# Rational layer's last units: f32 output product and another order of the element-wise steps

## The chip, the cores and the metric

One core of one Trainium2 chip runs the whole program as a single launch. The metric is the time on the device in microseconds (us). The engines are TensorE (PE, with its weight loads PEld), VectorE (DVE), ScalarE (ACT), GpSimd (POOL) and SyncE (SP).

## The reference, cut to what matters

```python
X = np.fft.fft(np.fft.fft(x, axis=1), axis=2).real      # x: 8 x 3072 x 256
x = X.reshape(24576, 256)
# mixture of 8 experts, one expert for each row, F = 1024
out[mask] = gate_w[mask, None] * (np.maximum(xe @ w1[e], 0.0) @ w2[e])
# rational layer
h = x @ w_in                                            # 256 -> 2048
P = a[0] + a[1] * h + a[2] * h2 + a[3] * h3
Q = 1.0 + np.abs(b[0]) * np.abs(h) + np.abs(b[1]) * h2
return (P / (Q + 1e-06)) @ w_out                        # 2048 -> 256
```

## The kernel before

After the transform and the sorting of rows by expert come two layers that run interleaved. The expert layer works in 103 blocks of 256 rows, each block in four "pieces" (two for the first product, two for the second). The rational layer works in 96 blocks of 256 rows, each in four "units" of 512 hidden columns, counted here by their place in the list `units`, 0 to 384; the last one is cut into two halves, 383 and 384. One round of the main loop issues one unit and one piece. The pieces end before unit 376, the value of `free`, so that units 376 to 384 have the engines to themselves: this is the stretch that the change touches, with 376 itself only at its border.

A unit i has these steps. `m2a(i)`: PE forms the hidden tile h (24 matmuls of 256 columns, f16 in high and low parts) in PSUM; ACT reads h three times, for a scaled absolute value (Abs), a square (Square) and a linear function (Identity); POOL adds the first two to q; DVE makes the numerator with two operations on the linear factor u and h (L1314, L1315). `m2b(i)`: ACT takes the logarithm of q (Ln) and its reciprocal (Exp, L1324), which it writes over h in PSUM; DVE finishes with three operations (L1325 to L1327). `m2g(i)`: ACT rounds the result to f16 (`ghi`), POOL makes the rest (`glo`). `m2c(i)`, three rounds later: PE multiplies both by the f16 parts of the output weights (24 matmuls of 256 columns) into the accumulator `po`; after a block's last unit `po` goes to `o` and by an indirect DMA to the output.

What sets the order is the text: the schedule is written by hand, each engine takes its instructions in that order, and waits are put in from what is read and written. h lives in one of three PSUM places: two turns of the tag `h2`, which units 376, 377, 378, 380, 381, 383 and 384 use, and one of the tag `h1` (units 379 and 382). So the matmuls of 378 reuse the place of 376, two units earlier, and those of 380 and later units the place of three units earlier. The u tiles by number: u__47327 is unit 376, u__47395 is 377, u__47478 is 378, u__47554 is 379, u__47627 to u__47765 are 380 to 382, u__47829 and u__47890 the halves 383 and 384.

Of the kernel before, what the change touches and what calls it, by code (L numbers as in the profile page):

```python
# [10 lines left out]
F32 = mybir.dt.float32  # L11
# [3 lines left out]
AF = mybir.ActivationFunctionType  # L15
ALU = mybir.AluOpType
# [4 lines left out]
P = 128  # L21
S = 3072
D = 256
# [108 lines left out]
def fourier_moe_rational_kernel(ctx, tc, xl, wg, w1, w2, w_in, w_out, av, bv, cst, out):  # L132
    nc = tc.nc
    V = nc.vector
# [23 lines left out]
    wslot = [keep.tile([P, wrow], F16, name=f"wslot{i}") for i in range(2)]  # L158
# [82 lines left out]
    with ExitStack() as c1:  # L241
# [53 lines left out]
        fs = spare[0][0:B, 1792:2816].rearrange("p (t c) -> p t c", t=4)  # L295
# [470 lines left out]
        for s in range(NS):  # L766
            p = s - 1
# [22 lines left out]
            else:  # L790
                parts = stage1_odd(b, eo, 3)
# [54 lines left out]
            parts = None  # L846
            if s and jh == 0:
                parts = stage1_odd(b, eo, 2)
# [29 lines left out]
        p = NS - 1  # L878
# [30 lines left out]
        for e in range(E):  # L909
            q = (nc.sync, nc.scalar)[e % 2]  # L910
            v = q.value_load(runi[0:1, e:e + 1], min_val=e * R, max_val=e * R + NT)
            ins_z.append(q.dma_start(out=xs[ds(v, TB), :], in_=cst["c_z"]))
        for i in ins_z:
# [25 lines left out]
                        op=ALU.is_ge)  # L939
# [7 lines left out]
                               op0=ALU.mult, op1=ALU.add)  # L947
# [10 lines left out]
        def places(k, end):  # L958
# [32 lines left out]
                        in1=sm[:, 8:16].unsqueeze(1).to_broadcast(bl), op=ALU.is_equal)  # L991
# [25 lines left out]
    wout = kp.tile([P, 2, 16, D], F16, name="wout")  # L1017
# [125 lines left out]
    st = {}  # L1143
# [40 lines left out]
    def three(ps, wa, wb, xa, xb):  # L1184

        n = len(wa)
        for i in range(n):
            nc.tensor.matmul(ps, lhsT=wa[i], rhs=xa[i], start=i == 0, stop=False)  # L1188
            nc.tensor.matmul(ps, lhsT=wb[i], rhs=xa[i], start=False, stop=False)  # L1189
        for i in range(n):  # L1190
            nc.tensor.matmul(ps, lhsT=wa[i], rhs=xb[i], start=False, stop=i == n - 1)  # L1191
# [95 lines left out]
        V.reciprocal(out=ir, in_=r)  # L1287
        nc.gpsimd.tensor_scalar(out=oj_, in0=ir, scalar1=ir, scalar2=og, op0=ALU.mult, op1=ALU.mult)

    def m2a(j, u, fs=range(4)):  # L1290
        yt = st["y", j][0]

        i = 4 * j + u + np_ - 4 * NSB + (fs[0] > 0)
        own = i < 1 or i % 3
        n = len(fs)
        ps = (psH if own else psM).tile([P, 4, TB], F32, tag="h2" if own else "h1", name="h2")[:, 0:n]
        for f in fs:
            fo = (4 * u + f) * P
            three(ps[:, f - fs[0]], [win[:, 0, kc, fo:fo + P] for kc in range(2)],
                  [win[:, 1, kc, fo:fo + P] for kc in range(2)],  # L1300
                  [yt[:, kc] for kc in range(2)], [yt[:, 2 + kc] for kc in range(2)])
        ab_ = tp.tile([P, 4, TB], F32, tag="ab", name="ab_")[:, 0:n]
        sq_ = tp.tile([P, 4, TB], F32, tag="sq", name="sq_")[:, 0:n]
        if i < 0:
            u_ = tp.tile([P, 4, TB], F32, tag="u", name="u_")
        else:

            u_ = bp.tile([P, 8, TB], F16, tag=("hhi", "hlo")[i % 2], name="u_")
            u_ = u_.rearrange("p f t -> p (f t)").bitcast(F32).rearrange("p (f t) -> p f t", t=TB)[:, 0:n]
        nc.scalar.activation(out=ab_, in_=ps, func=AF.Abs, scale=kb0)  # L1310
        nc.scalar.activation(out=sq_, in_=ps, func=AF.Square, scale=kb1)
        nc.scalar.activation(out=u_, in_=ps, func=AF.Identity, scale=ka3, bias=ka2)
        (V if fs[0] else nc.gpsimd).tensor_tensor(out=sq_, in0=sq_, in1=ab_, op=ALU.add)
        V.tensor_tensor(out=u_, in0=u_, in1=ps, op=ALU.mult)  # L1314
        V.scalar_tensor_tensor(out=u_, in0=u_, scalar=ka1, in1=ps, op0=ALU.add, op1=ALU.mult)  # L1315
        st["r", j, u, fs] = (ps, sq_, u_)

    def m2b(j, u, fs=range(4)):
        ps, q_, w_ = st["r", j, u, fs]
        n = len(fs)  # L1320
        L = tp.tile([P, 4, TB], F32, tag="L", name="L")[:, 0:n]
        nc.scalar.activation(out=L, in_=q_, func=AF.Ln, bias=c1b)

        nc.scalar.activation(out=ps, in_=L, func=AF.Exp, scale=-1.0, bias=st["bnd", j][3])  # L1324
        V.scalar_tensor_tensor(out=w_, in0=w_, scalar=a0, in1=ps, op0=ALU.add, op1=ALU.mult)  # L1325
        V.scalar_tensor_tensor(out=ps, in0=q_, scalar=C1, in1=ps, op0=ALU.add, op1=ALU.mult)  # L1326
        V.scalar_tensor_tensor(out=w_, in0=ps, scalar=st["bnd", j][5], in1=w_, op0=ALU.subtract, op1=ALU.mult,  # L1327
                               reverse0=True)

    def m2g(j, u, fs=range(4)):  # L1330
        ps, q_, w_ = st.pop(("r", j, u, fs))
        n = len(fs)
        ghi = tp.tile([P, 4, TB], F16, tag="ghi", name="ghi", bufs=3)[:, 0:n]
        glo = tp.tile([P, 4, TB], BF16, tag="glo", name="glo", bufs=3)[:, 0:n]
        nc.scalar.activation(out=ghi, in_=w_, func=AF.Copy)  # L1335
        (V if fs[0] else nc.gpsimd).tensor_tensor(out=glo, in0=w_, in1=ghi, op=ALU.subtract)  # L1336
        st["g", j, u, fs] = (ghi, glo)

    def m2c(j, u, fs=range(4)):
        ghi, glo = st.pop(("g", j, u, fs))  # L1340
        if u == 0:
            st["po", j] = psM.tile([P, 2, D], F32, tag="po", name="po")
        ps = st["po", j]
        for g, parts in ((ghi, (0, 1)), (glo, (0,))):
            for f in fs:
                for q in range(2):
                    for h in parts:
                        nc.tensor.matmul(ps[:, q], lhsT=g[:, f - fs[0], q * P:(q + 1) * P], rhs=wout[:, h, 4 * u + f],  # L1348
                                         start=g is ghi and u == 0 and f == 0 and q == 0 and h == 0,
                                         stop=g is glo and u == 3 and f == 3, skip_group_check=True)  # L1350
        if u == 3 and fs[-1] == 3:
            o = bp.tile([P, 2, D], F32, tag="o", name="o")
            oj_ = st.pop(("bnd", j))[7]
            t = st.pop(("y", j))[1]
            if j < NB - 1:
                nc.scalar.activation(out=o, in_=ps, func=AF.Copy, scale=oj_)
            else:
                V.tensor_scalar(out=o[:, 0], in0=ps[:, 0], scalar1=oj_, scalar2=None, op0=ALU.mult)
                nc.scalar.activation(out=o[:, 1], in_=ps[:, 1], func=AF.Copy, scale=oj_)
            for q in range(2):  # L1360
                ins = nc.gpsimd.indirect_dma_start(  # L1361
                    out=out, out_offset=bass.IndirectOffsetOnAxis(ap=t[:, q:q + 1], axis=0),
                    in_=o[:, q], in_offset=None, bounds_check=NT - 1, oob_is_err=False).ins
                tc.declare_no_dep(ins, group="out", reason="every token has a row of its own")
                tc.add_to_no_dep_group("out", ins)

    def piece(i, first=False):

        j, s_ = divmod(i, 4)
        if j >= NSB:  # L1370
            return
        if s_ == 0:
            pairs(j + 1, 1)
        if s_ < 2:
            m1a(j, s_, first)
        else:
            m1b(j, s_ - 2, first)
        if s_ == 3:
            pairs(j + 2, 0)
        if s_ == 3 and j + 2 < NSB:  # L1380
            gather(j + 2)
        if s_ == 1 and j + 1 < NSB:
            transp(j + 1)
        if s_ == 1 and j + 3 < NSB:
            load(j + 3)
# [34 lines left out]
    units = [(j, u) for j in range(NB) for u in range(4)]  # L1420
    last = units.pop()
    units += [(*last, range(2)), (*last, range(2, 4))]
    free = 4 * NSB - np_
    CL = 3
    for i in range(len(units) + CL + 1):

        lag = 1 + (i > free)
        if i == len(units):
            m2g(*units[i - lag])
        if 1 <= i <= len(units):  # L1430
            m2b(*units[i - 1])
        if i == len(units) - 1:
            m2g(*units[i - lag])
        if i < len(units):
            j, u = units[i][:2]
            if i == 0:
                piece(np_)
            m2a(*units[i])
            if i < len(units) - 1:
                if i:  # L1440
                    piece(i + np_)
                if u == 1 and j + 1 < NB:
                    bound_sum(j + 1)
                if u == 3 and j + 1 < NB:
                    bound_scale(j + 1)
                if u == 1 and j + 1 < NB:
                    load_y(j + 1)
        if i not in (free + 1, len(units) - 1, len(units)) and lag <= i < len(units) + lag:
            m2g(*units[i - lag])
        if i < len(units) - 1:  # L1450
            if u == 1 and j + 1 < NB:
                bound(j + 1)
            if u == 3 and j + 2 < NB:
                bound_rows(j + 2)
            if u == 1 and j:
                bound_out(j)
        if CL <= i < len(units) + CL:
            m2c(*units[i - CL])
# [35 lines left out]
```

## Time and profile before

| what | value |
|---|---|
| median of 3 runs | 3513.91 us (3513.57 to 3516.85) |
| profiled execution: time, span | 3516.32 us, 3514.6 us |
| busy over the span: PE, DVE, ACT, POOL | 96%, 87%, 89%, 80% |
| mean granted TensorE clock | 0.984 of full speed |

The span runs from the first to the last instruction of the profiled execution; the time holds in addition what lies around it. Busy shares are averages over the whole span, and say nothing of the last units by themselves.

### The profile page before, as it was taken

The page shows a single profiled execution, that of the slowest core. Times are in us where ns is not written, and L with a number is a line of the kernel's source. Part 1 is how long each engine was busy: PE and PEld are TensorE (multiplying, and loading weights), DVE is VectorE, ACT ScalarE, POOL GpSimd, SP SyncE. Part 2 cuts the span into 40 slices and gives each one's busy share as a digit, 9 for nine tenths or more (in the row PEclk, how much of TensorE's full clock was granted, in tenths as well). Part 3 has the DMA queues.
Part 4 walks back from the last instruction along what each step waited for, and adds up shares of the span by engine and source line. Part 5 has one row for each costly group of instructions (what it writes and reads, how often), then busy time and mean ns, then how long its engine had stood idle before and what let it go on. Part 6 is the DMA issues. An engine that isn't in the chain of part 4 may idle for free.

```text
span 3514.6 us, 75025 instructions
## 1 busy us (share of the span) xinstructions
PE 3391.1 (96%) x29902; PEld 2968.8 (84%) x29902; DVE 3044.7 (87%) x3214; ACT 3123.4 (89%) x3904; POOL 2824.1 (80%) x2552
## 2 busy tenths in 40 slices
PE   7984989999999999999999999999999999999997
PEld 5663778888888888888888888888888888888885
DVE  9986668888988889888988889888898888888897
ACT  4774479999999999999999999999999999999997
POOL 2887668888888888888888888888888888888876
PEclk9996999999999999999999999999999999999999
DMA  8987423111321123111221123111311123212110
GB/s 298 305 274 261 105 43 93 38 43 45 67 70 40 43 43 94 39 45 43 67 69 40 42 45 93 44 40 43 91 46 40 44 43 91 46 40 43 44 31 19
DMA packets 344639, 268.32 MB, mean 76 GB/s; under 512 B 182470, under 2 KB 319686, under 8 KB 337232
## 3 DMA queue, kind: packets, MB, share of 16 engines
q1 hardware_dynamic: 311136, 182.50, 21.7%
q0 software_dynamic: 33024, 79.96, 6.6%
q8 instruction: 234, 3.83, 0.6%
q14 instruction: 117, 0.96, 0.2%
q10 hardware_dynamic: 128, 1.06, 0.1%
HBM read 327.00 MB, written 96.92 MB: 121 GB/s over the span
## 4 chain that ended last, share of the span: by engine, by line
PE 88%; DVE 4%; ACT 2%; issue 2%; DMA 2%; POOL 1%; POOLq 0%; SPq 0%; ACTq 0%; DVEq 0%
PE po L1348 28%; PE h L1189 14%; PE h L1188 14%; PE h L1191 14%; PE py L1191 5%; PE py L1188 5%; PE py L1189 5%; POOL xs L612 1%; DMA xs<-y,sli 1%; PE ps L507 1%; PE pq L531 1%; PE ps L480 1%; PE pq L532 1%; DVE h L1326 0%; ACT h L1324 0%
## 5 line engine op out<-in xcount | busy, mean ns | idle before, releaser
L1188 PE MATMUL h<-yr,win 128*128 128x256 f16 x3072 | 755.7, 273 | 8.9 <-DVE u__5102 L1327 5.6
L1189 PE MATMUL h<-yr,win 128*128 128x256 f16 x3072 | 755.7, 273 | 0.0
L1348 PE MATMUL po<-wout,ghi 128*128 128x256 f16 x6144 | 735.1, 273 | 11.2 <-ACT ghi L1335 7.6
L1348 PEld LDWEIGHTS <-ghi 128*128 128x128 f16 x6144 | 593.6, 98 | 81.7 <-ACT ghi L1335 12.0
L1191 PE MATMUL h<-yr,win 128*128 128x256 f16 x3072 | 587.5, 273 | 0.0
L1324 ACT ACTIVATE h<-L,bnd 128x1024 f32<-128x1024 f32 x385 | 429.6, 1116 | 20.9 <-DVE u__47829 L1315 1.5
L1188 PE MATMUL h<-xt,wslot 128*128 128x256 f16 x1648 | 406.3, 274 | 2.5 <-DVE hlo L1214 1.7
L1189 PE MATMUL h<-xt,wslot 128*128 128x256 f16 x1648 | 406.3, 274 | 0.0
L1348 PE MATMUL po<-wout,glo 128*128 128x256 f16 x3072 | 399.3, 273 | 1.8 <-POOL glo L1336 1.8
L1188 PE MATMUL py<-hhi,wslot 128*128 128x256 f16 x1648 | 373.4, 274 | 3.5 <-ACT hhi L1208 3.5
L1189 PE MATMUL py<-hhi,wslot 128*128 128x256 f16 x1648 | 373.3, 274 | 0.0
L1189 PEld LDWEIGHTS <-wslot 128*128 128x128 f16 x3296 | 323.5, 98 | 45.1 <-issue 6.9
L1188 PEld LDWEIGHTS <-wslot 128*128 128x128 f16 x3296 | 323.3, 98 | 39.1 <-issue 0.4
L1191 PEld LDWEIGHTS <-wslot 128*128 128x128 f16 x3296 | 323.1, 98 | 38.5 <-issue 0.3
L1188 PEld LDWEIGHTS <-win 128*128 128x128 f16 x3072 | 300.7, 98 | 45.5 <-DVE u__5102 L1327 5.7
L1348 PEld LDWEIGHTS <-glo 128*128 128x128 bf16 x3072 | 300.4, 98 | 38.4 <-POOL glo L1336 3.2
L1189 PEld LDWEIGHTS <-win 128*128 128x128 f16 x3072 | 301.0, 98 | 35.2
L1191 PEld LDWEIGHTS <-win 128*128 128x128 f16 x3072 | 300.8, 98 | 35.2
L612 POOL DMA_INDIRECT xs<-y,sli x192 | 225.5, 1175 | 117.1 <-ACT L L535 58.5
L1191 PE MATMUL h<-xt,wslot 128*128 128x256 f16 x1648 | 315.8, 273 | 0.0
L1214 DVE SCALAR_TENSOR_TENSOR hlo<-h,hhi 128x1024 f16<-128x1024 f32 x197 | 240.0, 1218 | 29.1 <-ACT hhi L1208 24.1
L1361 POOL DMA_INDIRECT out_dram<-o,id x192 | 199.3, 1038 | 53.7 <-issue 47.3
(4924 smaller groups left out, 9119.7 us busy)
## 6 DMA issues: line engine op xcount, KB each, us to landing
xr<-xs SPq DMA_DIRECT2D x103, 258.0 KB, 2.9
ys<-yw SPq DMA_DIRECT2D x103, 256.0 KB, 5.5
yr<-ys SPq DMA_DIRECT2D x96, 256.0 KB, 3.8
xh<-x_l SPq DMA_DIRECT2D x14, 1536.0 KB, 9.2
wf<-in_moe_w_dram SPq DMA_DIRECT2D x16, 1024.0 KB, 6.6
ws<-wh SPq DMA_DIRECT2D x16, 1024.0 KB, 12.1
xh<-in_moe_w_in_dram SPq DMA_DIRECT2D x4, 1024.0 KB, 5.9
wslot<-ws SPq DMA_DIRECT2D x4, 1024.0 KB
```

What stands on the lines that cost most here:

```text
L480: nc.tensor.matmul(ps[0:m, 0:n], lhsT=eo[i][:, jh, c], rhs=mat[:, c, 0:n], start=c == 0, stop=c == 2)
L507: nc.tensor.matmul(ps[q][0:m, 0:NH], lhsT=eo[i][:, c], rhs=mat[:, c], start=c == 3 * q, stop=c == 3 * q + 2)
L531: nc.tensor.matmul(pq[:, k, 0:NC], lhsT=u[2 * par][:, js], rhs=rc, start=True, stop=False)
L532: nc.tensor.matmul(pq[:, k, 0:NC], lhsT=u[2 * par + 1][:, js], rhs=rs, start=False, stop=True)
L612: ins = nc.gpsimd.indirect_dma_start(out=xs, out_offset=bass.IndirectOffsetOnAxis(ap=sli[:, t0 + t:t0 + t + 1], axis=0), in_=y[:, t], in_o ...
L1188: nc.tensor.matmul(ps, lhsT=wa[i], rhs=xa[i], start=i == 0, stop=False)
L1189: nc.tensor.matmul(ps, lhsT=wb[i], rhs=xa[i], start=False, stop=False)
L1191: nc.tensor.matmul(ps, lhsT=wa[i], rhs=xb[i], start=False, stop=i == n - 1)
L1214: V.scalar_tensor_tensor(out=hlo[:, sl], in0=ps, scalar=0.0, in1=hhi[:, sl], op0=ALU.max, op1=ALU.subtract)
L1324: nc.scalar.activation(out=ps, in_=L, func=AF.Exp, scale=-1.0, bias=st["bnd", j][3])
L1348: nc.tensor.matmul(ps[:, q], lhsT=g[:, f - fs[0], q * P:(q + 1) * P], rhs=wout[:, h, 4 * u + f], start=g is ghi and u == 0 and f == 0 and ...
L1361: ins = nc.gpsimd.indirect_dma_start(out=out, out_offset=bass.IndirectOffsetOnAxis(ap=t[:, q:q + 1], axis=0), in_=o[:, q], in_offset=None, ...
```

## The change

For the units after 376 three things differ. The result of a unit is no longer split: the f32 tile u goes into the output product as it is, against f32 weights `w32`, which POOL adds up from the two f16 parts in four operations (`widen`) in rounds 376 to 379, into the weight slot that the last odd expert block has left. ACT forms the linear factor first, DVE makes the numerator from it at once, and only then comes Abs. Between Abs and Square of unit i stands the whole of `m2b(i - 1)`, which before stood ahead of `m2a(i)`.

```diff
@@ m2a @@
+        st["r", j, u, fs] = (ps, sq_, u_)
+
+        def numerator():
+            V.tensor_tensor(out=u_, in0=u_, in1=ps, op=ALU.mult)
+            V.scalar_tensor_tensor(out=u_, in0=u_, scalar=ka1, in1=ps, op0=ALU.add, op1=ALU.mult)
+
+        if between is not None:
+            nc.scalar.activation(out=u_, in_=ps, func=AF.Identity, scale=ka3, bias=ka2)
+            numerator()
         nc.scalar.activation(out=ab_, in_=ps, func=AF.Abs, scale=kb0)
+        if between is not None:
+            between()
         nc.scalar.activation(out=sq_, in_=ps, func=AF.Square, scale=kb1)
-        nc.scalar.activation(out=u_, in_=ps, func=AF.Identity, scale=ka3, bias=ka2)
+        if between is None:
+            nc.scalar.activation(out=u_, in_=ps, func=AF.Identity, scale=ka3, bias=ka2)
         (V if fs[0] else nc.gpsimd).tensor_tensor(out=sq_, in0=sq_, in1=ab_, op=ALU.add)
-        V.tensor_tensor(out=u_, in0=u_, in1=ps, op=ALU.mult)
-        V.scalar_tensor_tensor(out=u_, in0=u_, scalar=ka1, in1=ps, op0=ALU.add, op1=ALU.mult)
-        st["r", j, u, fs] = (ps, sq_, u_)
+        if between is None:
+            numerator()
...
+    w32 = wslot[1].bitcast(F32)
+
+    def widen(q):
+        nc.gpsimd.tensor_tensor(out=w32[:, 1024 * q:1024 * q + 1024].rearrange("p (k d) -> p k d", d=D),
+                                in0=wout[:, 0, 4 * q:4 * q + 4], in1=wout[:, 1, 4 * q:4 * q + 4], op=ALU.add)
+
     def m2g(j, u, fs=range(4)):
         ps, q_, w_ = st.pop(("r", j, u, fs))
+        if 4 * j + u > free:
+            st["g", j, u, fs] = (w_, None)
+            return
...
@@ m2c @@
+        if glo is None:
+            for f in fs:
+                k = (4 * u + f) * D
+                for q in range(2):
+                    nc.tensor.matmul(ps[:, q], lhsT=ghi[:, f - fs[0], q * P:(q + 1) * P], rhs=w32[:, k:k + D],
...
@@ the main loop @@
-        if 1 <= i <= len(units):
+        late = free < i < len(units)
+        if 1 <= i <= len(units) and not late:
             m2b(*units[i - 1])
...
-            m2a(*units[i])
+            m2a(*units[i], between=(lambda: m2b(*units[i - 1])) if late else None)
...
+        if free <= i < free + 4:
+            widen((i + 1) % 4)
```

The order on ACT, before, in the round of unit 378 (h_47451, u__47478; sq__47394 and h_47368 are unit 377, u__47327 is 376). In brackets stand the engines whose progress an instruction waits for:

```order
L1322 ACTIVATE L<-sq__47394,c1b 128x1024 [waits Pool_49]
L1324 ACTIVATE h_47368<-L,bnd 128x1024 [waits DVE_49,Activation_49]
L1310 ACTIVATE ab__47476<-h_47451,coef 128x1024 [waits PE_49]
L1311 ACTIVATE sq__47477<-h_47451,coef 128x1024
L1312 ACTIVATE u__47478<-h_47451,coef 128x1024
L1335 ACTIVATE ghi<-u__47327 128x1024
```

The order on ACT after, in the same round (h_47447, u__47474 are unit 378; sq__47389 and h_47363 are unit 377; L1317 is the Identity, L1319 Abs, L1333 Ln, L1335 Exp, L1322 Square):

```order
L1317 ACTIVATE u__47474<-h_47447,coef 128x1024 [waits PE_49]
L1319 ACTIVATE ab__47472<-h_47447,coef 128x1024 [waits DVE_49]
L1333 ACTIVATE L<-sq__47389,c1b 128x1024 [waits Pool_49]
L1335 ACTIVATE h_47363<-L,bnd 128x1024 [waits Activation_49]
L1322 ACTIVATE sq__47473<-h_47447,coef 128x1024
L1355 ACTIVATE ghi<-u__47327 128x1024
```

Identity has moved to the head of the round, Ln and Exp of unit 377 from ahead of the three reads to between Abs and Square, and Abs, which waited for PE, waits for DVE.

The order on DVE, before, from the end of unit 377 to the start of the end of unit 378:

```order
L1325 SCALAR_TENSOR_TENSOR u__47395<-u__47395,a_3464,h_47368 128x1024 [waits Activation_49]
L1326 SCALAR_TENSOR_TENSOR h_47368<-sq__47394,h_47368 128x1024 [waits Pool_49]
L1327 SCALAR_TENSOR_TENSOR u__47395<-h_47368,bnd,u__47395 128x1024 [waits DVE_49]
L1314 TENSOR_TENSOR u__47478<-u__47478,h_47451 128x1024 [waits PE_49,Activation_49]
L1315 SCALAR_TENSOR_TENSOR u__47478<-u__47478,coef,h_47451 128x1024 [waits DVE_49]
L1325 SCALAR_TENSOR_TENSOR u__47478<-u__47478,a_3464,h_47451 128x1024 [waits Activation_49]
```

The order on DVE after, from the numerator of unit 378 (L1313, L1314) over the end of unit 377 (L1336 to L1338) to the numerator of unit 379:

```order
L1313 TENSOR_TENSOR u__47474<-u__47474,h_47447 128x1024 [waits Activation_49]
L1314 SCALAR_TENSOR_TENSOR u__47474<-u__47474,coef,h_47447 128x1024 [waits DVE_49]
L1336 SCALAR_TENSOR_TENSOR u__47390<-u__47390,a_3464,h_47363 128x1024 [waits Activation_49]
L1337 SCALAR_TENSOR_TENSOR h_47363<-sq__47389,h_47363 128x1024 [waits Pool_49]
L1338 SCALAR_TENSOR_TENSOR u__47390<-h_47363,bnd,u__47390 128x1024 [waits DVE_49]
L1313 TENSOR_TENSOR u__47551<-u__47551,h_47524 128x1024 [waits Activation_49]
```

The numerator of a unit now stands ahead of the last three operations of the unit before it; the five operations of a unit are the same.

## Rows read from the trace of the kernel before

**Rows 1.** Windows: us; busy PE, PEld, DVE, ACT, POOL; granted clock; DMA share, GB/s.

```profile
3440.00:3505.00 65.00, 49.29 (x407) 40.07 (x408) 52.79 (x50) 51.97 (x60) 42.45 (x31) 0.95 0.05 13
```

**Rows 2.** Timeline of DVE, one unit: start, length, operation, [idle before].

```profile
3459.21 1.28 DVE L1325 SCALAR_TENSOR_TENSOR u__47478<-u__47478,a,h 128x1024 f32<-128x1024 f32 x1 [1.25 <-ACT h L1324]
3460.41 1.22 DVE L1326 SCALAR_TENSOR_TENSOR h<-sq__47477,h 128x1024 f32<-128x1024 f32 x1
3461.66 1.28 DVE L1327 SCALAR_TENSOR_TENSOR u__47478<-h,bnd,u__47478 128x1024 f32<-128x1024 f32 x1
3462.86 1.21 DVE L1314 TENSOR_TENSOR u__47554<-u__47554,h 128x1024 f32<-128x1024 f32 x1
3464.11 1.28 DVE L1315 SCALAR_TENSOR_TENSOR u__47554<-u__47554,coef,h 128x1024 f32<-128x1024 f32 x1
3466.64 1.28 DVE L1325 SCALAR_TENSOR_TENSOR u__47554<-u__47554,a,h 128x1024 f32<-128x1024 f32 x1 [1.25 <-ACT h L1324]
```

**Rows 3.** Timeline of ACT, the same unit.

```profile
3459.11 1.10 ACT L1310 ACTIVATE ab__47552<-h,coef 128x1024 f32<-128x1024 f32 x1
...
3461.11 1.20 ACT L1312 ACTIVATE u__47554<-h,coef 128x1024 f32<-128x1024 f32 x1
...
3463.72 1.13 ACT L1322 ACTIVATE L<-sq__47553,c1b 128x1024 f32<-128x1024 f32 x1
3465.49 1.12 ACT L1324 ACTIVATE h<-L,bnd 128x1024 f32<-128x1024 f32 x1 [0.63 <-DVE u__47554 L1315]
```

**Rows 4.** Timeline of DVE: unit 376's numerator and end, 382's end.

```profile
3441.82 1.28 DVE L1315 SCALAR_TENSOR_TENSOR u__47327<-u__47327,coef,h 128x1024 f32<-128x1024 f32 x1
...
3446.80 1.28 DVE L1327 SCALAR_TENSOR_TENSOR u__47327<-h,bnd,u__47327 128x1024 f32<-128x1024 f32 x1
...
3491.68 1.28 DVE L1327 SCALAR_TENSOR_TENSOR u__47765<-h,bnd,u__47765 128x1024 f32<-128x1024 f32 x1
```

**Rows 5.** Timeline of PE: first and last matmuls of unit 377, first of 378.

```profile
3440.71 0.28 PE L1188 MATMUL h<-yr,win 128*128 128x256 f16 x1 [1.08 <-DVE u__47211 L1327]
...
3443.12 0.38 PE L1191 MATMUL h<-yr,win 128*128 128x256 f16 x2
...
3448.14 0.28 PE L1188 MATMUL h<-yr,win 128*128 128x256 f16 x1 [1.97 <-DVE u__47327 L1327]
```

**Rows 6.** Timeline of PE, second transform stage: f32 matmuls of 273 columns.

```profile
63.30 0.62 PE L531 MATMUL pq<-wslot,u 128*128 128x273 f32 x2
...
64.22 0.62 PE L531 MATMUL pq<-wslot,u 128*128 128x273 f32 x2
...
298.58 1.28 PE L531 MATMUL pq<-wslot,u 128*128 128x273 f32 x2 [6.13 <-ACT L L535]
```

**Rows 7.** Windows behind two idle stretches of PE (columns as in the first group).

```profile
298.50:300.50 2.00, 1.92 (x4) 1.51 (x5) 1.54 (x6) 0.93 (x5) 1.28 (x3) 0.50 1.00 393
3486.40:3489.80 3.40, 3.33 (x16) 2.31 (x16) 2.12 (x3) 2.81 (x5) 3.06 (x2) 0.50 0.00 0
```

**Rows 8.** Timeline of POOL: the sum of one unit.

```profile
3468.72 2.37 POOL L1313 TENSOR_TENSOR sq__47626<-sq__47626,ab__47625 128x1024 f32<-128x1024 f32 x1 [2.69 <-ACT sq__47626 L1311]
```

**Rows 9.** Timeline of the half units 383 and 384, DVE and ACT.

```profile
3496.55 0.75 DVE L1327 SCALAR_TENSOR_TENSOR u__47829<-h,bnd,u__47829 128x512 f32<-128x512 f32 x1
3497.28 1.62 DVE L1313 TENSOR_TENSOR sq__47889<-sq__47889,ab__47888 128x512 f32<-128x512 f32 x1
3498.83 0.68 DVE L1314 TENSOR_TENSOR u__47890<-u__47890,h 128x512 f32<-128x512 f32 x1
...
3502.50 0.75 DVE L1327 SCALAR_TENSOR_TENSOR u__47890<-h,bnd,u__47890 128x512 f32<-128x512 f32 x1
...
3498.94 0.72 ACT L1322 ACTIVATE L<-sq__47889,c1b 128x512 f32<-128x512 f32 x1 [0.50 <-DVE sq__47889 L1313]
```

**Rows 10.** Timeline of the end: the two halves of the last output tile.

```profile
3505.57 0.48 DVE L1358 TENSOR_SCALAR o<-po,bnd 128x256 f32<-128x256 f32 x1 [0.85 <-PE po L1348]
3506.09 0.47 ACT L1359 ACTIVATE o<-po,bnd 128x256 f32<-128x256 f32 x1 [2.10 <-DVE o L1358]
```

More of the change, by code (lines that the diff above doesn't have):

```diff
@@ L1288, in bound_out, with m2a @@
         nc.gpsimd.tensor_scalar(out=oj_, in0=ir, scalar1=ir, scalar2=og, op0=ALU.mult, op1=ALU.mult)
-    def m2a(j, u, fs=range(4)):
+    def m2a(j, u, fs=range(4), between=None):
         yt = st["y", j][0]
@@ L1343, in m2c @@
         ps = st["po", j]
-        for g, parts in ((ghi, (0, 1)), (glo, (0,))):
+        if glo is None:
[3 more added lines that the diff above has]
+                    nc.tensor.matmul(ps[:, q], lhsT=ghi[:, f - fs[0], q * P:(q + 1) * P], rhs=w32[:, k:k + D],
+                                     start=u == 0 and f == 0 and q == 0, stop=u == 3 and f == 3,
+                                     skip_group_check=True)
+        for g, parts in ((ghi, (0, 1)), (glo, (0,))) if glo is not None else ():
             for f in fs:
@@ L1429, in fourier_moe_rational_kernel @@
             m2g(*units[i - lag])
-        if 1 <= i <= len(units):
+        late = free < i < len(units)
+        if 1 <= i <= len(units) and not late:
             m2b(*units[i - 1])
-        if i == len(units) - 1:
-            m2g(*units[i - lag])
         if i < len(units):
@@ L1447, in fourier_moe_rational_kernel @@
                     load_y(j + 1)
-        if i not in (free + 1, len(units) - 1, len(units)) and lag <= i < len(units) + lag:
+        if i not in (free + 1, len(units)) and lag <= i < len(units) + lag:
             m2g(*units[i - lag])
+        if free <= i < free + 4:
+            widen((i + 1) % 4)
         if i < len(units) - 1:
```

## The prediction, made before the changed kernel ran

> **What bounds the kernel now.** The table of busy shares has PE at 96%, so for most of the span PE is the limit; none of that time is touched. The change acts only on the last units, so the view to read is the window of that stretch, and then the timelines inside it. In the window [rows 1] no engine is full: DVE works 52.79 of 65.00 us, ACT 51.97, PE 49.29. Something passes between engines.
>
> The timeline of DVE shows what. A unit takes 7.43 us, from one L1325 at 3459.21 to the next at 3466.64; it holds five operations that follow each other closely, and one idle time of 1.25 us, which Exp ended [rows 2]. The timeline of ACT shows the other side: Exp at 3465.49 waited for DVE's L1315 [rows 3], because it writes over h, which the numerator reads. So the cycle is: last three operations of unit i (3.65 us, 3459.21 to 3462.86), numerator of unit i + 1 (2.53 us, 3462.86 to 3465.39), then Exp of i + 1 (1.12 us, and about 0.1 us of hand-over), all in a ring. Units 376 to 382 keep to it: their ends lie 44.88 us apart for six units, 7.48 each [rows 4].
>
> **The change, part by part.** The sum is made against the profiled execution (3516.32 us, span 3514.6) as a difference, and added to the median of 3513.91 us, which lies 2.41 us lower.
>
> *The ring.* After the change DVE's list is numerator(i), end(i - 1), numerator(i + 1). Exp(i - 1) no longer has to wait for a numerator just made, which would take the 1.25 us away. But ACT's list is Identity(i), Abs(i), Ln(i - 1), Exp(i - 1), Square(i), and Abs now waits for DVE. The only new DVE work ahead of it on its h is the numerator. Everything behind Abs on ACT waits with it, and DVE's next work, end(i - 1), needs Exp. So DVE stands idle for Abs, Ln and Exp in turn. Abs takes 1.00 us to the next start (3459.11 to 3461.11 for two), Ln 1.13, of which the next operation can overlap 0.1, and Exp 1.12 [rows 3]: with two hand-overs of 0.04 us, 3.25 us. One unit then takes 2.53 + 3.25 + 3.65 = 9.43 us instead of 7.43: 2.0 us more. Identity(i + 1) comes 2.1 us after Exp(i - 1) has started end(i - 1), inside its 3.65 us, and adds nothing.
>
> Does an engine that reads PSUM wait for another that only reads? The row that bears on it is the last one: ACT's half of `o` waited 2.10 us and began at 3506.09, just after DVE's half, which began at 3505.57 and took 0.48, though the two read different halves of `po`, and neither writes what the other reads [rows 10]. So yes; the price here is the numerator's full length. The Trainium skill, page "PSUM — Partial Sum Buffer", section "PSUM bank collisions raise a hardware error", says that two engines must not touch the same bank at once, reads against reads too, and that a dependency is put between them. By that rule Abs has to wait as in the sum; without it the sum would be that of the first rival.
>
> *Entry, unit 376.* Before, its numerator ended at 3443.10, Exp followed, and its end came at 3448.08 [rows 4]. Now numerator(377) and Abs stand ahead. The matmuls of 377 end at 3443.50 [rows 5]; Identity 1.20, numerator 2.53, the three ACT steps 3.25, the end 3.73 (to its very end) and hand-overs give 3454.25: **+6.2 us**.
>
> *Unit 377.* The matmuls of 378 need the h place of 376, as they do now: they waited 1.97 us for its end [rows 5]. Before, this was hidden, since end(377) did not stand behind unit 378. Now it does: after the end of 376 come 24 matmuls (2.78 us, 3440.71 to 3443.50), Identity 1.20, numerator 2.53, ACT 3.25, end 3.73, together 13.6 us instead of 7.43: **+6.2 us**. PE has then been idle for some 8 us. Behind 6.13 us of idle time a pair of f32 calls took 1.28 us, against 0.62 elsewhere [rows 6], at a granted clock of 0.50 [rows 7], the lower level of 1.2 GHz. At that clock the 24 matmuls take 2.6 us longer: I take **+2.5 us**, from bounds of 0 and 2.6.
>
> *Units 378 to 381.* Their h places come from three units back or from the other tag, so the ring rules: 4 x 2.0 = **+8.0 us**.
>
> *The halves.* End(382) stands behind a half numerator and a half Abs, some 1.5 us shorter: 7.9 us against 7.43, **+0.5**. End(383): numerator 1.45, ACT steps about 1.85, hand-overs 0.1, end 2.1 are 5.5, against 4.34 (3492.96 to 3497.30), **+1.1**. End(384) finds its numerator done: sum, Ln 0.72, Exp about 0.7, end 2.1. The sum took 1.62 us beside POOL's work; POOL is now free, and the nearest row is the 0.68 us of L1314 [rows 9]. I take 0.7: 4.1 us against 5.95 (3497.30 to 3503.25), **-1.85**; with 1.62 it is -0.9.
>
> *The output product.* In f32 one call is two records, and two calls follow at 0.92 us, 0.46 for 273 columns [rows 6], so 0.43 for 256. Eight calls cost 3.5 us in place of 24 x 0.109 = 2.6 (the spacing of the matmuls of h, [rows 5]); with the matmuls of h PE has 6.1 us per unit, under 9.43. Only the last product is on the path: four calls with the tail of the last, 1.9 us, against 2.32 from the end of 384 to the start of `o` (3503.25 to 3505.57 [rows 9, 10]), where ghi, glo and 12 matmuls stood: **-0.35 us**. At half clock it is +1.4.
>
> *Edits at nothing.* The split that goes away (ghi on ACT, glo on POOL) stood beside DVE's ring. The four `widen` steps lie on POOL in rounds 376 to 379. No row has an f16 addition of that size; the nearest is the sum at 2.37 us [rows 8], the bounds are 0 and some 5. In the walk each sum stands ready 3.8 us or more before its Ln, which covers twice 2.37 a round; beyond that the rest would be added, up to four times.
>
> Sum: 6.2 + 6.2 + 2.5 + 8.0 + 0.5 + 1.1 - 1.85 - 0.35 = 22.3 us, so 3513.9 + 22.3 = **3536 us**.
>
> **The rivals.** *Abs is not held* (not slower). If Abs(i) reads h beside the numerator, Ln and Exp are done while DVE is still busy, the ring goes, and a unit takes DVE's own 6.18 us. Entry and unit 377 still lose 3.5 us each, for the moved numerator and the h place; units 378 to 381 gain 2.2 in all (378 and 379 still fill), the halves 4.6, the end 0.35, and the clock costs 2.5: about +2, **3516 us**. For it: the split and the ring are gone; against it: the wait at Abs, and the ACT row of the last group. It decides when end(i - 1) starts within 0.2 us of the end of numerator(i).
>
> *PE becomes the bound.* At the lower clock h and f32 product take twice 6.1, 12.2 us per unit; over 9.43 that is 2.8 more for five units: 22 + 14, **3550 us**. For it: each unit leaves PE some 3 us idle, and one such wait of before was followed by a window at 0.50, from 3486.40 [rows 7]. Against it: PE then fills its idle time and has its full clock back after a few us, as in the window of before, whose mean is 0.95 [rows 1].
>
> **How the numbers follow.** The forecast, a slower kernel by the ring, has 0.85; Abs not held 0.08; PE as the bound 0.07. A measurement can tell 0.2%, 7.0 us, from no change. The forecast's own ends: without the clock term and with entry and unit 377 a little shorter, +15; with the clock low in some units and at the end, +30. This gives 3529 to 3544, which holds 0.8. Slower takes the forecast and PE as the bound, 0.92; the first rival gives same 0.07, and 0.01 for faster, if its fill costs less.
>
> **What would show it.** In the trace of after: DVE idle about 3.2 us ahead of every L1336, released by Exp, and Abs released by L1314; ends of units 9.4 us apart, the first two 13 to 16; PE at 0.50 behind 3454; f32 calls at 0.43 us. I am wrong if Abs starts before L1314 has ended, if the ring is under 8 us, or if PE, not ACT, ends DVE's waits.

## The result, and the profile after

The changed kernel took 3539.03 us (median of 4 runs, 3537.74 to 3539.96), the kernel before 3515.38 us (4 runs on the same chip): a ratio of 1.0064, with a 95% interval of 1.0052 to 1.0076, 23.65 us slower by the medians. The profiled execution has a span of 3538.2 us against 3514.6.

The last units in the timeline of DVE after, one unit long, answer to [rows 2]; L1336 to L1338 are the three closing operations, L1313 and L1314 the numerator:

```profile
3484.49 1.28 DVE L1336 SCALAR_TENSOR_TENSOR u__47551<-u__47551,a,h 128x1024 f32<-128x1024 f32 x1 [3.37 <-ACT h L1335]
3485.69 1.22 DVE L1337 SCALAR_TENSOR_TENSOR h<-sq__47550,h 128x1024 f32<-128x1024 f32 x1
3486.94 1.28 DVE L1338 SCALAR_TENSOR_TENSOR u__47551<-h,bnd,u__47551 128x1024 f32<-128x1024 f32 x1
3488.14 1.21 DVE L1313 TENSOR_TENSOR u__47669<-u__47669,h 128x1024 f32<-128x1024 f32 x1
3489.39 1.28 DVE L1314 SCALAR_TENSOR_TENSOR u__47669<-u__47669,coef,h 128x1024 f32<-128x1024 f32 x1
3494.04 1.28 DVE L1336 SCALAR_TENSOR_TENSOR u__47621<-u__47621,a,h 128x1024 f32<-128x1024 f32 x1 [3.37 <-ACT h L1335]
```

The five operations last as before; the idle time ahead of the closing ones has grown from 1.25 to 3.37 us, and a unit from 7.43 to 9.55 us. The timeline of ACT for the same unit answers to [rows 3]:

```profile
3485.39 1.20 ACT L1317 ACTIVATE u__47669<-h,coef 128x1024 f32<-128x1024 f32 x1
3490.71 1.11 ACT L1319 ACTIVATE ab__47667<-h,coef 128x1024 f32<-128x1024 f32 x1 [4.13 <-DVE u__47669 L1314]
3491.72 1.14 ACT L1333 ACTIVATE L<-sq__47620,c1b 128x1024 f32<-128x1024 f32 x1
3492.89 1.12 ACT L1335 ACTIVATE h<-L,bnd 128x1024 f32<-128x1024 f32 x1
3493.94 1.09 ACT L1322 ACTIVATE sq__47668<-h,coef 128x1024 f32<-128x1024 f32 x1
```

Identity is done at 3486.59, and then ACT stands idle for 4.13 us: Abs starts only at 3490.71, when L1314 has ended (3490.67). Ln and Exp follow without a gap, DVE's L1336 0.03 us after Exp. At the start of the stretch, PE waits for the h place of unit 376; the timeline of PE answers to [rows 5]:

```profile
3453.39 0.40 PE L1188 MATMUL h<-yr,win 128*128 128x256 f16 x1 [8.31 <-DVE u__47327 L1338]
```

Behind that idle time its granted clock, the third number from the right in a window, is 0.50, the lower of the two levels (columns as in [rows 1]; it answers to [rows 7]):

```profile
3453.40:3457.30 3.90, 3.90 (x19) 2.80 (x20) 0.00 (x0) 0.00 (x0) 3.39 (x7) 0.50 0.02 4
```

At the end the products of units 383 and 384, four f32 calls in eight records each, meet another stretch at the lower clock, and the last output tile waits for the second of them. First the timeline of PE ([rows 10] is the same place before):

```profile
3521.11 2.54 PE L1368 MATMUL po<-wslot,u__47763 128*128 128x256 f32 x8 [1.88 <-DVE u__47763 L1338]
3525.36 3.78 PE L1368 MATMUL po<-wslot,u__47800 128*128 128x256 f32 x8 [1.71 <-DVE u__47800 L1338]
```

The timeline of DVE at the last output tile:

```profile
3529.18 0.48 DVE L1385 TENSOR_SCALAR o<-po,bnd 128x256 f32<-128x256 f32 x1 [3.87 <-PE po L1368]
```

And three windows: the first and a later part of 383's product, and the eight records of 384's. The clock is 1.00 right behind the 1.88 us of idle time, falls within 383's product, and is 0.50 for all of 384's:

```profile
3521.10:3522.10 1.00, 0.99 (x5) 0.89 (x6) 0.55 (x1) 0.41 (x1) 0.00 (x0) 1.00 0.00 0
3522.50:3523.00 0.50, 0.50 (x2) 0.34 (x2) 0.00 (x0) 0.50 (x1) 0.00 (x0) 0.50 0.00 0
3525.40:3529.10 3.70, 3.70 (x8) 2.45 (x8) 0.00 (x0) 0.00 (x0) 0.00 (x0) 0.50 0.00 0
```

### The profile page after: what moved, and what is told of

Read it like the earlier page. It is cut to its first block, busy times and chain, and to the rows that moved or that the text cites. A ratio compares the mean times of both kernels' runs of the same rounds, so it can differ in the third digit from the quotient of the medians.

```text
span 3538.2 us, 74876 instructions
## 1 busy us (share of the span) xinstructions
PE 3400.3 (96%) x29846; PEld 2976.6 (84%) x29846; DVE 3043.4 (86%) x3213; ACT 3115.5 (88%) x3896; POOL 2817.6 (80%) x2549
## 4 chain that ended last, share of the span: by engine, by line
PE 85%; DVE 2%; ACT 2%; issue 2%; POOL 1%; DMA 1%; POOLq 0%; SPq 0%; ACTq 0%; DVEq 0%
PE po L1375 27%; PE h L1188 14%; PE h L1189 14%; PE h L1191 14%; PE py L1188 5%; PE py L1189 5%; PE py L1191 5%; POOL xs L612 1%; DMA xs<-y,sli 1%; DMA ws<-wh 0%; DVE h L1337 0%; DMA wslot<-ws,widx 0%; ACT h L1335 0%; ACT L L1333 0%; POOL win L1073 0%
## 5 line engine op out<-in xcount | busy, mean ns | idle before, releaser
L1188 PE MATMUL h<-yr,win 128*128 128x256 f16 x3072 | 757.7, 274 | 20.7 <-DVE u__47327 L1338 8.3
L1375 PE MATMUL po<-wout,ghi 128*128 128x256 f16 x6032 | 721.4, 273 | 4.5 <-ACT o L1383 4.5
L1375 PEld LDWEIGHTS <-ghi 128*128 128x128 f16 x6032 | 583.4, 98 | 71.9 <-ACT ghi L1355 4.2
L1335 ACT ACTIVATE h<-L,bnd 128x1024 f32<-128x1024 f32 x385 | 429.6, 1116 | 15.3 <-ACT L L1333 0.3
L1375 PE MATMUL po<-wout,glo 128*128 128x256 f16 x3016 | 390.9, 273 | 0.0
L1214 DVE SCALAR_TENSOR_TENSOR hlo<-h,hhi 128x1024 f16<-128x1024 f32 x197 | 240.0, 1218 | 28.6 <-ACT hhi L1208 23.6
```

The lines of the kernel that those rows point to most:

```text
L1214: V.scalar_tensor_tensor(out=hlo[:, sl], in0=ps, scalar=0.0, in1=hhi[:, sl], op0=ALU.max, op1=ALU.subtract)
```

## The experiments

Two theories. **A:** Abs, held until the numerator has read h, keeps Ln and Exp of the unit before from starting, and so makes the ring of 9.5 us; the second unit's loss comes from the h place that it shares with the first. **B:** the loss comes with the f32 product, which costs PE more and holds the u tile longer.

What differs between these kernels is the last 60 to 90 us, and what lies ahead of it shifts by some us from one execution to the next (the numerator of 376 ends at 3442.00 after and at 3443.10 before; in e5 to e10 it ended 21 to 27 us later than before, and the kernel before, run beside them, took 3542.49 us (e5 to e8) and 3541.0 us (e9, e10)). So the table gives, beside the ratio to the kernel before run beside it, a *stretch* read from the timeline of DVE: from the end of unit 376's numerator to the start of the last output tile. The units' columns are the distances between the ends of their last closing operations (for 376 from the end of its numerator); "end" is from the last of these to the output tile. The stretch of the changed kernel begins at the end of this operation (timeline of DVE, after) and ends at the output tile shown above:

```profile
3440.72 1.28 DVE L1314 SCALAR_TENSOR_TENSOR u__47327<-u__47327,coef,h 128x1024 f32<-128x1024 f32 x1
```

The diffs below are against the changed kernel where nothing else is said.

| kernel | ratio (95% interval) | stretch | 376 | 377 | 378 | 379 | 380 | 381 | 382 | 383 | 384 | end |
|---|---|---|---|---|---|---|---|---|---|---|---|---|
| before | 1 | 62.47 | 4.98 | 7.43 | 7.43 | 7.43 | 7.73 | 7.43 | 7.43 | 4.34 | 5.95 | 2.32 |
| after | 1.0064 (1.0052 to 1.0076) | 87.18 | 11.32 | 15.80 | 9.55 | 9.55 | 9.55 | 9.62 | 8.05 | 5.61 | 4.25 | 3.88 |
| e1 | 1.0006 (0.9997 to 1.0015) | 66.48 | 8.87 | 13.00 | 7.34 | 7.79 | 6.10 | 6.15 | 6.12 | 3.43 | 4.25 | 3.43 |
| e2 | 1.0065 (1.0051 to 1.0079) | 87.28 | 11.32 | 15.86 | 9.55 | 9.55 | 9.56 | 9.61 | 8.06 | 5.61 | 5.84 | 2.32 |
| e3 | 0.9999 (0.999 to 1.0008) | 62.18 | 4.98 | 7.43 | 7.43 | 8.69 | 7.43 | 7.43 | 7.43 | 4.33 | 4.94 | 2.09 |
| e4 | 1.0048 (1.0034 to 1.0061) | 80.98 | 11.32 | 9.61 | 9.56 | 9.55 | 9.55 | 9.61 | 8.06 | 5.61 | 4.25 | 3.86 |
| e5 | 1.0 (0.999 to 1.001) | 64.58 | 8.64 | 12.81 | 6.87 | 8.04 | 6.10 | 6.15 | 6.12 | 3.50 | 4.26 | 2.09 |
| e6 | 0.9986 (0.9976 to 0.9996) | 60.82 | 8.88 | 6.20 | 7.44 | 9.85 | 6.09 | 6.15 | 6.11 | 3.75 | 4.25 | 2.10 |
| e7 | 0.9993 (0.9983 to 1.0004) | 62.83 | 9.87 | 7.15 | 7.14 | 7.14 | 7.14 | 7.15 | 6.03 | 3.62 | 4.26 | 3.33 |
| e8 | 0.9992 (0.9983 to 1.0001) | 62.80 | 9.88 | 7.14 | 7.15 | 7.14 | 7.15 | 7.14 | 6.04 | 3.63 | 5.21 | 2.32 |
| e9 | 0.999 (0.9981 to 0.9998) | 57.90 | 8.87 | 6.21 | 7.46 | 7.02 | 6.09 | 6.16 | 6.11 | 3.64 | 4.25 | 2.09 |
| e10 | 1.0001 (0.9991 to 1.0012) | 62.21 | 8.87 | 6.20 | 7.35 | 7.50 | 6.94 | 7.28 | 6.24 | 3.43 | 6.08 | 2.32 |

### e1: Abs ahead of Identity

```diff
+        nc.scalar.activation(out=ab_, in_=ps, func=AF.Abs, scale=kb0)
         if between is not None:
             nc.scalar.activation(out=u_, in_=ps, func=AF.Identity, scale=ka3, bias=ka2)
             numerator()
-        nc.scalar.activation(out=ab_, in_=ps, func=AF.Abs, scale=kb0)
         if between is not None:
             between()
```

> The changed kernel with one line moved: Abs stands ahead of Identity and the numerator instead of behind them, all else as it is. Theory A (Abs, held until the numerator has read h, keeps Ln and Exp of the unit before from starting): VectorE's 3.4 us ahead of the first closing operation fall under 1 us, units 378 to 381 end 6.2 to 7.5 us apart instead of 9.55, and the time falls by 15 to 21 us, to 3518 to 3524. Theory B (the f32 product makes PE, or the u tile that it holds, the limit): within 3 us of the changed kernel's 3539.

One line moved takes back 20.7 of the 24.7 us: the stretch is 66.48 us and the median 3519.56. The distances of units 378 to 381 miss the expected 6.2 to 7.5 us at both edges (7.34, 7.79, 6.10 and 6.15). Units 380 to 382 take 6.10 to 6.15 us, DVE's own work. Timeline of ACT in unit 382's round, e1:

```profile
3481.25 1.11 ACT L1316 ACTIVATE ab__47717<-h,coef 128x1024 f32<-128x1024 f32 x1
3482.25 1.22 ACT L1318 ACTIVATE u__47719<-h,coef 128x1024 f32<-128x1024 f32 x1
3483.84 1.15 ACT L1333 ACTIVATE L<-sq__47668,c1b 128x1024 f32<-128x1024 f32 x1 [0.38 <-POOL sq__47668 L1325]
3485.02 1.12 ACT L1335 ACTIVATE h<-L,bnd 128x1024 f32<-128x1024 f32 x1
3486.39 1.11 ACT L1322 ACTIVATE sq__47718<-h,coef 128x1024 f32<-128x1024 f32 x1 [0.26 <-DVE u__47719 L1314]
```

The timeline of DVE beside it:

```profile
3485.08 1.28 DVE L1314 SCALAR_TENSOR_TENSOR u__47719<-u__47719,coef,h 128x1024 f32<-128x1024 f32 x1
3486.28 1.28 DVE L1336 SCALAR_TENSOR_TENSOR u__47669<-u__47669,a,h 128x1024 f32<-128x1024 f32 x1
```

Ln and Exp now run while DVE is at the numerator, and L1336 follows it at 3486.28. Square, which still reads h behind Identity, now is the one that waits for L1314, but only 0.26 us, and nothing that DVE needs soon stands behind it. The 13.00 us of unit 377 stay: theory A's second half.

### e2: the order alone, e3: the f32 product alone

e2 keeps the split:

```diff
-        if 4 * j + u > free:
-            st["g", j, u, fs] = (w_, None)
-            return
...
-        if free <= i < free + 4:
-            widen((i + 1) % 4)
```

> The new order of the element-wise steps alone: the result of a unit is split into f16 parts and multiplied in 24 matmuls as before, and the f32 weights are not made. Theory A: the ring of 9.5 us stays, since nothing of it is in the product; 3535 to 3543. Theory B: the loss goes with the f32 product; 3513 to 3519.

One small thing beside the order differs from before in e2, as in e8 and e10: the split of unit 382 stands behind `m2a(384)` instead of ahead of it. The change moves it, though the shortened diff does not show that; in the changed kernel, where 382 is not split, it has no effect.

e3 keeps the f32 product, and has the order of before:

```diff
-        late = free < i < len(units)
-        if 1 <= i <= len(units) and not late:
+        if 1 <= i <= len(units):
...
-            m2a(*units[i], between=(lambda: m2b(*units[i - 1])) if late else None)
+            m2a(*units[i], between=None)
```

> The f32 output product alone, with the four additions that make its weights; the element-wise steps in the order of before. Theory A: units 7.4 us apart as before, and a gain or loss of at most 3 us at the end, where the last product stands in place of the split; 3512 to 3519. Theory B: 3533 to 3542.

The two halves of the change separate cleanly: the order alone has the whole loss (87.28 us; up to 383 every unit within 0.06 us of the changed kernel), the f32 product alone none (62.18). Behind 383 the sums agree by two terms that offset each other: in e2 unit 384 is 1.59 us longer, since DVE's sum runs beside POOL, and the end 1.56 shorter, at full clock. Theory B falls. e3 also shows the f32 product at the end at full clock; the timeline of PE:

```profile
3499.03 1.99 PE L1368 MATMUL po<-wslot,u__47806 128*128 128x256 f32 x8 [0.21 <-DVE u__47806 L1338]
```

The window of these records:

```profile
3499.00:3501.00 2.00, 1.97 (x8) 1.44 (x8) 0.00 (x0) 0.00 (x0) 0.00 (x0) 1.00 0.00 0
```

The same eight records as in the changed kernel, 1.99 us instead of 3.78: PE had come from 383's product after 0.21 us of idle time, there the clock had already fallen within 383's product. In e3 the additions for the weights do cost something, 1.25 us in unit 379: DVE waits 2.50 us, because Ln waited for POOL. Timeline of ACT, e3:

```profile
3461.34 1.15 ACT L1333 ACTIVATE L<-sq__47556,c1b 128x1024 f32<-128x1024 f32 x1 [2.69 <-POOL sq__47556 L1325]
```

And of DVE, e3:

```profile
3463.67 1.28 DVE L1336 SCALAR_TENSOR_TENSOR u__47557<-u__47557,a,h 128x1024 f32<-128x1024 f32 x1 [2.50 <-ACT h L1335]
```

### e4: the places of h dealt in threes

```diff
-        own = i < 1 or i % 3
+        own = i < 1 or i % 3 != 2
```

> The changed kernel with the places of h dealt otherwise: units 378, 381 and 384 take the tag h1, so that every unit from 378 on reuses the place of three units earlier and 378 no longer waits for 376. If the second unit's 15.8 us come from that place and from the clock that PE loses while it waits (theory A's account), unit 377 ends 9.5 us behind 376 and the time falls by 5 to 8 us, to 3531 to 3534. If they come from the order alone (any unit that enters it loses as much), or from the f32 product (theory B), within 2 us of 3539.

Unit 377 falls from 15.80 to 9.61 us, a ring like the others, and nothing else changes: 6.2 us of stretch, median 3533.31. The two ends in the timeline of DVE, e4:

```profile
3455.16 1.28 DVE L1338 SCALAR_TENSOR_TENSOR u__47327<-h,bnd,u__47327 128x1024 f32<-128x1024 f32 x1
3464.77 1.28 DVE L1338 SCALAR_TENSOR_TENSOR u__47390<-h,bnd,u__47390 128x1024 f32<-128x1024 f32 x1
```

With e1 this is the second half of theory A.

### e5: Abs in its place, but reading another tile

```diff
+        av_ = ps if between is None else win[:, 0, 0, 0:n * TB].rearrange("p (f t) -> p f t", t=TB)
-        nc.scalar.activation(out=ab_, in_=ps, func=AF.Abs, scale=kb0)
+        nc.scalar.activation(out=ab_, in_=av_, func=AF.Abs, scale=kb0)
```

> The changed kernel with every instruction where it is, but Abs of the units after 376 reads part of the f16 input weights in SBUF instead of h, so that the absolute value of h is left out there. Theory A says that it is the shared read of h that holds Abs, not its place in ScalarE's list: Abs then follows Identity at once, VectorE's 3.4 us ahead of the first closing operation fall under 1 us, and from the end of unit 376's numerator to the start of the last output tile it takes 64 to 69 us, as with Abs moved to the front (66.5), instead of 87.2. The rival, that one more ScalarE operation between the numerator's input and Ln is what costs, keeps it at 84 to 88.

With every instruction in the place of the changed kernel the stall is gone (64.58 us), so it is not the place of Abs in ACT's list but the shared h. Timeline of ACT, e5:

```profile
3478.99 1.21 ACT L1317 ACTIVATE u__47474<-h,coef 128x1024 f32<-128x1024 f32 x1 [6.96 <-PE h L1191]
3480.09 1.14 ACT L1320 ACTIVATE ab__47472<-win,coef 128x1024 f32<-128x1024 f16 x1
3481.13 1.14 ACT L1334 ACTIVATE L<-sq__47389,c1b 128x1024 f32<-128x1024 f32 x1
```

DVE's L1337, the first closing operation in this kernel's lines, waits 0.69 us, as it does in units 376 to 378. Two waits are not under the 1 us that was expected, 1.78 us in 379, where Ln waits 0.98 us for POOL's sum, and 1.00 in 382. Timeline of DVE, e5:

```profile
3483.45 1.28 DVE L1337 SCALAR_TENSOR_TENSOR u__47390<-u__47390,a,h 128x1024 f32<-128x1024 f32 x1 [0.69 <-ACT h L1336]
```

### e6 to e10: versions without the ring

e6 is e1 and e4 together, by the diffs above. e7 is e6 with Square moved as well:

```diff
         nc.scalar.activation(out=ab_, in_=ps, func=AF.Abs, scale=kb0)
+        nc.scalar.activation(out=sq_, in_=ps, func=AF.Square, scale=kb1)
         if between is not None:
             nc.scalar.activation(out=u_, in_=ps, func=AF.Identity, scale=ka3, bias=ka2)
             numerator()
         if between is not None:
             between()
-        nc.scalar.activation(out=sq_, in_=ps, func=AF.Square, scale=kb1)
```

e8 is e7, and e10 is e6, with the split of e2's diff. e9 is e6 with the f32 product from unit 376 on:

```diff
-        if 4 * j + u > free:
+        if 4 * j + u >= free:
...
-            widen((i + 1) % 4)
+            widen(i % 4)
```

> Abs ahead of Identity and the places of h dealt in threes, together: both losses of the change that the runs have shown apart (the ring, and the second unit's wait for the place of the first) are taken away, the f32 product stays. If the two add up, 20.7 and 6.2 us off 87.2, the stretch from unit 376's numerator to the last output tile takes 59 to 62 us, against 62.5 of before. If the ring's stall was what the place's wait hid behind, so that they do not add, 64 to 66.

The two losses add: 60.82 us, and a kernel that is a little faster than before (0.9986; 1.65 us by its stretch). That the sum comes out to 0.5 us is partly luck: against e1, unit 379 is 2.06 us longer and the end 1.33 shorter.

> As the run with Abs first and places in threes, and Square ahead of Identity as well, so that all three reads of h stand ahead of the numerator and no ScalarE read waits for VectorE. GpSimd's sum then comes earlier and Ln no longer waits for it (0.4 to 1.1 us in each of four units with Abs first alone): 58 to 61 us for the same stretch, and 1 to 3 us less than the run beside it. If the later Identity delays the numerator as much as Ln gains, no difference.

A miss: 62.83 us, 2 us more than e6, and units 377 to 381 all at 7.14 or 7.15. A new ring has come, which the expectation did not see. Timeline of ACT, e7:

```profile
3504.33 1.09 ACT L1316 ACTIVATE ab__47717<-h,coef 128x1024 f32<-128x1024 f32 x1
3507.14 1.11 ACT L1317 ACTIVATE sq__47718<-h,coef 128x1024 f32<-128x1024 f32 x1 [1.72 <-DVE h L1337]
```

The operation that it waited for, in the timeline of DVE:

```profile
3505.88 1.22 DVE L1337 SCALAR_TENSOR_TENSOR h<-sq__47620,h 128x1024 f32<-128x1024 f32 x1
```

Square of unit 382 writes the tile that q of unit 380 still fills (sq has two turns, and the number 47620 is two units back), and waits for DVE's last read of it, L1337. Identity and the numerator stand behind it. In e6 Square stood later and waited for L1314 instead, 0.42 us at most. No run gave sq a third turn. Against e6 the ring costs 1.0 us in each of units 380 and 381; but up to the end of 384 e7 is only 0.8 us behind, since e6 has its 9.85 us in unit 379, and the other 1.2 us lie in the end, 3.33 against 2.10 us, where e7's last product fell to the lower clock (0.71, then 0.50 in the windows from 3529.50 and 3531.00).

> The three reads first and places in threes, with the f16 split and the 24 matmuls in place of the f32 product. If the f32 product is worth nothing once the ring is gone, the stretch is within 2 us of the run with it. If ScalarE (a sixth operation in each unit) or GpSimd (the rest, 2.1 us) then sets the unit's time, it is 3 to 8 us longer.

With that ring the split costs nothing in the units up to 383, which agree within 0.01 us. That the whole stretch does too, 62.80 us, is luck: unit 384 takes 0.95 us more, and the end, which in e7 was at the lower clock, 1.01 less.

> The run with Abs first and places in threes, but unit 376 too gives its result unsplit to the f32 product, and the four additions come in the order in which the units need them. In that run unit 378 took 9.9 us where its neighbours took 6.1 to 7.4: the matmuls of 380 stood behind the product of 376, which waited 2.5 us for its f16 rest, behind GpSimd's small operations, and ran into the lower clock. If that is the cause, 378 falls to 6.1 to 7.5 us, and the stretch from unit 376's numerator to the last output tile from 60.8 to 57 to 59 us. If the places or the additions on GpSimd are the cause, it stays at 60 to 62.

e9 is the fastest by its stretch, 57.90 us, 4.6 less than before; unit 379 falls from 9.85 to 7.02. (The expectation named 378 for the unit of 9.9 us, which by its end is 379.) Its ratio is 0.999 (0.9981 to 0.9998), 4.4 us between the medians. What is gone is this chain of e6: the second half of 376's product waits for its f16 rest (timeline of PE, e6),

```profile
3486.24 1.24 PE L1375 MATMUL po<-wout,glo 128*128 128x256 f16 x8 [2.50 <-POOL glo L1356]
```

the matmuls of 380 stand behind it, and ACT's first read of 380, with Identity and the numerator behind it, waits for them (timeline of ACT, e6):

```profile
3491.61 1.11 ACT L1316 ACTIVATE ab__47619<-h,coef 128x1024 f32<-128x1024 f32 x1 [3.45 <-PE h L1191]
```

> Abs first and places in threes with the f16 split and its 24 matmuls, no f32 product: what the f32 product is worth once the ring is gone and ScalarE's list is the better one. If nothing but the end (a sum beside GpSimd's work, 0.9 to 1.6 us), the stretch takes 61 to 63 us against 60.8 with it. If the sixth ScalarE operation or the rest on GpSimd holds each unit, 65 to 70.

The f32 product is worth 1.4 us beside e6 (62.21 against 60.82) and 4.3 beside e9: units 380 and 381 take 6.94 and 7.28, since ghi stands ahead of the next reads on ACT, and the sum of 384 runs beside POOL (2.51 us). Unit 379, with no additions for the weights, is 2.35 us shorter, though 376 is still split: so the additions, which stand ahead of 376's rest on POOL in e6, are part of the chain that e9 took away, and e9 alone does not tell the two apart.

## Why the prediction was right, step by step

The mechanism and its size held: 22.3 us were forecast. In the two profiled executions the stretch grew by 24.71 us (62.47 to 87.18), and began 1.10 us earlier, which gives the 23.6 us between the spans. That the spans differ by less than the stretches is an accident of the two executions.

- **The ring**: 9.43 us forecast, 9.55 measured; the idle time was 3.37 us for 3.25. (The terms as written add up to 3.23; the 0.1 us by which Exp was to overlap Ln did not come: Exp starts 1.17 us behind Ln's start, not 1.03.) That Abs waits for a numerator that only reads was taken from [rows 10] and the order; e5 shows it, since Abs from another tile starts at once. The rule of the Trainium skill's page "PSUM — Partial Sum Buffer", section "PSUM bank collisions raise a hardware error", that reads against reads get a dependency too, is thereby borne out by this case as far as the wait goes: a read is held for another engine's read. What would happen without the wait was not tried.
- **Entry, unit 376**: +6.2 forecast, 11.32 - 4.98 = +6.3 measured. Of this, 3.7 us or more stay in each version that puts the numerator of 377 ahead of 376's end, even where nothing holds Abs (e5, 8.64 us; e1 and e6 to e10, 8.87 to 9.88).
- **Unit 377**: +6.2 and +2.5 for the clock forecast, 15.80 - 7.43 = +8.4 measured. The clock was at 0.50, the lower of the two levels, for the first 4 us behind 8.31 us of idle time, and the last of the 24 matmuls ran at full clock again: they took 4.64 us (3453.39 to 3458.03) against 2.64 before (3448.14 to 3450.78), so the clock's share was 2.0, not 2.5 us. e4 shows the cause: with another place for h both the wait and the lower clock behind it are gone from that unit. The list of signs gave 13 to 16 us for the first two units, which does not agree with the sum's own 11.2 and 16.1; measured are 11.32 and 15.80.
- **Units 378 to 381**: +8.0 forecast; 38.27 against 30.02 is +8.25.
- **The halves**: +0.5, +1.1 and -1.85 forecast; +0.6, +1.3 and -1.7 measured. DVE's sum took 0.68 us with POOL free (e2, where the rest still runs on POOL: 2.27).
- **The output product at the end**: the mis-sized term. I took -0.35 and named +1.4 as what it would be at half clock; it was 3.88 - 2.32 = +1.56. The price of an f32 call was right (e3: 2.09 us for this place at full clock), the clock was not: the forecast took full clock at the end, and it fell within the product before, so that the last one ran at 0.50 throughout.
- **Edits at nothing**: `widen` took 2.1 us on POOL each, and cost nothing in this order. In the order of before it cost 1.25 us (e3), so the cover was the ring's own idle time. The prediction's 3.8 us alone would not have covered twice 2.37; POOL still stood idle 0.51 us or more ahead of each of the sums of 377 to 380.

Of the rivals, Abs not held is what e5 made of the kernel: 64.6 us, 2.1 above before, where I had worked out about 2. PE as the bound did not come: PE was busy 61.60 of 90 us between 3439 and 3529, with a mean clock of 0.83 (window of after), Exp ended each of DVE's waits for a closing operation, and in e2, with another product, the units were the same; PE's slow stretches lay beside the ring except at the two places above.

```profile
3439.00:3529.00 90.00, 61.60 (x354) 48.98 (x354) 51.16 (x49) 45.54 (x52) 36.69 (x28) 0.83 0.04 9
```

## What to carry to other kernels

When two engines read one PSUM tile, put the reads of the engine that has more work queued behind them first: here the later read of the same tile was held until the other engine's reads had ended, and all that was queued behind it waited too. Moving a step earlier on one engine moves its tile's other readers, its buffer turns and the list behind them; e1 and e7 each turn on one such line. Before a product is made cheaper in instructions, ask where it ends and at which clock: the last f32 product took 3.78 us at the lower level in the changed kernel, and 1.99 at full clock in e3.

## What the hardware showed that I had not expected

PE's clock fell while PE was at work again, behind idle times shorter than one that cost nothing. In the changed kernel unit 383's product began at 1.00 behind 1.88 us of idle time and was at 0.50 from 3522.50 on (windows above); in e1 and e7 the same came within 384's product, behind 1.99 and 1.93 us. Before, the last product came behind 3.28 us and ran its 1.5 us at full clock throughout, as the timeline of PE before shows,

```profile
3504.05 1.05 PE L1348 MATMUL po<-wout,ghi 128*128 128x256 f16 x8 [3.28 <-ACT ghi L1335]
```

and its window:

```profile
3504.00:3505.50 1.50, 1.45 (x12) 1.09 (x12) 0.69 (x1) 0.00 (x0) 0.00 (x0) 1.00 0.00 0
```

So in these rows the length of the last idle time alone does not say which clock follows. What does is open.

The kernel before needed 3515.8 us beside e1 to e4 and 3541 to 3542.5 us beside the later runs. In the traces of e1 and e6 the difference is 26.9 us at an early numerator (477.55 us in e1) and still 26.9 at 3388 us: so it arises ahead of 478 us, long before the stretch studied here. Its cause was not looked for.
